# VectorE's reciprocal for the memory rows' softmax factors, and row work moved behind them, in a segment-recurrent attention kernel

## The chip, the cores and the metric

One NeuronCore of a Trainium2 chip runs the whole program. The metric is the time of one execution in microseconds of the device. The kernel before takes 1620.86 us, the median of three executions (1619.89, 1620.86 and 1621.39 us).

## The reference

Four residual steps run over x of 2048 rows by 512 columns: attention with a carried memory (A), a spatially gated MLP (B), A again, B again. The change touches A alone. Cut to what matters:

```python
for s in range(n_seg):                       # 64 segments of 32 rows
    h = concatenate([mem, xs])               # 8 memory rows ahead of the 32 token rows
    q, k, v = h @ Wq, h @ Wk, h @ Wv         # 32 heads of 128 columns
    p = softmax(where(mask, q @ k.T * scale, -1e9))
    o = (p @ v) @ Wo                         # over all heads
    mem = o[:8]                              # the next segment's memory
    outs.append(o[8:])
```

A segment can't begin before the eight memory rows of the segment ahead of it have gone through the softmax, through p @ v and through Wo. There are two blocks A, so 128 segments in a row. In the last segment of each block nothing follows on the memory rows; 126 segments have a step for them.

## The kernel before, in words

**Tiling.** `a_block` builds one block A and calls `segment` 64 times. The 32 heads stand as two halves, r = 0 (heads 0 to 15) and r = 1 (heads 16 to 31). In each half, 8 pairs of heads fill 128 partitions, and a score tile has 224 columns. The tiles of a segment that matter here:

- `E[:, r]`: the masked exponentials of half r, written by VectorE in `close(r)` (L980).
- `psO[0]` and `psO[1]`: the products p @ v of the two halves in PSUM, written by TensorE in `pv(r)` (L1020, L1023). The tile of the second half also holds the sums of the exponentials for the memory rows: `sums[0]`, made ahead of `pv(0)` by `sums_ahead` (L1003), lies in columns 384 to 511 of the first bank of `psO[1]`; `sums[1]`, made after `pv(1)` by `sums_memory` (L994), lies in columns 320 to 383 of both banks. `pv(1)` therefore writes over the bank in which `sums[0]` stands.
- `Rm[:, r]`: the softmax factors 1/sum of the memory rows in SBUF, 128 partitions by 128 fp32 elements.
- `psT`: the sums of the token rows, made by `sums_tokens` (L1012). Their factors `Rt` come later, in `token_factors` (L1087, L1090).
- `uT`: the scaled rows as TensorE takes them for Wo, 32 heads wide.

**The step of the change** is `memory_out(r, ps)` at L1035. It takes the sums to their inverses by exp(-ln(sum)): a Ln on ScalarE from PSUM to `Rm` (L1037), then an Exp with scale -1 on `Rm` in place (L1038). VectorE then multiplies the eight memory rows of `psO[r]` by `Rm` into `uT` (L1039).

**Order of the work.** Each engine runs its instructions in the order in which the program text issues them (a manual schedule for TensorE, VectorE and ScalarE; the DMA issues of SyncE and GpSimd follow the text as well). There is no planner; the order is written out by hand in `segment`. Around the change it reads:

1. `exps(1)`, the copy of the second half's values to `VA` on VectorE (L1075), `close(1)`, then `spare0()`, a hook in which VectorE may do row work of the block's other stages.
2. `fill()` (TensorE work of other stages: projections `psb` of the next 128 rows, or rows of `pwB`), `sums_ahead`, `fill()`, `pv(0)`.
3. `memory_out(0, sums[0])`.
4. `spare1(E)`, a second hook with row work.
5. `pv(1)`, `sums_memory(1)`, `sums_tokens`.
6. `memory_out(1, sums[1])`.
7. `run(copies)` (ScalarE's evictions of the fill work), then `wo_pairs` (L808: heads 0 to 17 into `px`, 36 matmuls) and `wo_rest` (L815: heads 18 to 31 into a part of `psO[0]`). Heads 16 and up need `memory_out(1)`.
8. ScalarE's copy `cross` (L1132), `token_factors`, the hook `spare2`, VectorE's `fold` (L906, L909) and `build_hA` (L916, L917), which writes the memory rows of the next segment into `hT`. The next segment's projections `psQ`, `psm`, `psK`, `psV` (all L731) follow.

**What `spare1` holds.** By segment it is nothing, or one or two of: half of a row block's sum (`rows.y_half`, VectorE L240, with a store issued by GpSimd at L242) or half of its statistics (`y_stats`, VectorE L150); in every fourth segment the next row block's normalisation (`rows.apply`, VectorE L207, with a transposing DMA issued by SyncE at L211); in a few segments the release of finished rows (VectorE L1227 with a store by SyncE); near the end of a block also GpSimd's row sums (L230), and a memset (L1232) with a weight load by GpSimd.

Of the kernel before, what the change touches and what calls it, by code (L numbers as in the profile page):

```python
# [9 lines left out]
ACT = mybir.ActivationFunctionType  # L10
# [662 lines left out]
def a_block(tc, c, rows, front, MV_in, RS_in, MV_out, RS_out, ahead, wo, S, first):  # L673
    nc = tc.nc
    NSEG = S // SEG
    NB = S // P
    scale = float(DH) ** -0.5
    maskN, ones, half = c["maskN"], c["ones"], c["half"]

    with ExitStack() as ctx:  # L680
# [86 lines left out]
        def run(todo):  # L767
            while todo:
                todo.pop(0)()
# [101 lines left out]
        def y_stats(tb, k):  # L871

            if k == 0:
                halves[tb] = rows.pool.tile([P, 2, nc.vector.BN_STATS_DIM], F32, name="bnst2")
            _half_stats(nc, halves[tb], rows.y[tb][0], k, MV_out[:, tb, :])
            if k == 2:
                copies.append(lambda: _rstd_act(nc, RS_out[:, tb:tb + 1], MV_out[:, tb, 1:2], c))
# [47 lines left out]
        def segment(s, fill, spare0, spare1, spare2, spare3, tail, loads):  # L925
# [11 lines left out]
            E = segp.tile([P, 2, 2, 224], BF16, name="E", bufs=1)  # L937
# [88 lines left out]
            def oview(r, lo, hi):  # L1026
                return psO[r][:, :, 0:320].rearrange("p g (n q) -> p g n q", q=40)[:, :, :, lo:hi]

            def hview(t, r, lo, hi):
                return t.rearrange("p (r g n) q -> p r g n q", r=2, g=2)[:, r, :, :, lo:hi]  # L1030
# [3 lines left out]

            def memory_out(r, ps):  # L1035
                rm = Rm[:, r]
                nc.scalar.activation(out=rm, in_=ps, func=ACT.Ln)  # L1037
                nc.scalar.activation(out=rm, in_=rm, func=ACT.Exp, scale=-1.0)  # L1038
                nc.vector.tensor_tensor(out=hview(uT_cur[:], r, 24, 32), in0=oview(r, 0, 8), in1=rm.rearrange("p g (n q) -> p g n q", q=8), op=ALU.mult)  # L1039

            def tok_out(r):
# [41 lines left out]
            ends_here = s + 1 == NSEG  # L1083
            Rt = segp.tile([P, 2, 512], F32, name="Rt", tag="Rt", bufs=1)

            def token_factors(rs):
                nc.scalar.activation(out=Rt[:], in_=psT[:], func=ACT.Ln)  # L1087
                for r in rs:
                    rt = Rt[:, :, 256 * r:256 * r + 256]
                    nc.scalar.activation(out=rt, in_=rt, func=ACT.Exp, scale=-1.0)  # L1090

            def between():
                if first and s == 0:
                    fill()
                    run(turns)
# [7 lines left out]
            pv(0)  # L1103
            if not ends_here:
                memory_out(0, sums[0])
            spare1(E)
            between()
            pv(1)
            if not ends_here:
# [2 lines left out]
            if ends_here:  # L1112
                spare2()
                token_factors((1, 0))
            else:
                memory_out(1, sums[1])
            run(copies)
            px = accB.tile([P, 512], F32, name="px")
            pw = psO[0][:, 0, 384:512]
# [62 lines left out]
        def y_load(y, o):  # L1182
            rows.y_load(y, first, nc.gpsimd, rows.pool.tile([P, DM], F32, name="y_x")[:], o)()
# [8 lines left out]
        for s in range(NSEG):  # L1192
# [19 lines left out]
            def spare1(E):  # L1212
                for y, added in ys:
                    if added:
                        y_stats(y, 1)
                    elif tb < NB - 1:
                        if j4 < 3:
                            rows.y_half(y, first, 1, nc.gpsimd)
                    else:
                        nc.gpsimd.tensor_copy(seen[:], E[:, 1, 0, 0:1])  # L1220
                        rows.y_add(y, first, nc.gpsimd, nc.gpsimd)
                if s == NSEG - 1:
                    y_load(NB - 5, rows.pool.tile([P, DM], F32, name="y_o")[:])
                    rows.y_add(NB - 5, first, nc.gpsimd, nc.gpsimd)
                if stores and not ys:
                    last = yB[max(yB)][:, 0:1]
                    nc.vector.tensor_copy(last, last)  # L1227
                    run(stores)
                if j4 == 3 and tb + 2 < NB:
                    rows.apply(tb + 2, MV_in, RS_in, first=first)  # L1230
                if s == NSEG - 2:
                    nc.vector.memset(front.w_in_sb[:, 2, FH - 1:FH + 1], 0.0)  # L1232
                    front.load_w(2)

            def spare2():
                if first and s == 8:
                    c["cast_bsp"] = c["load_bsp"]()
                if first and s == 12:
                    c["cast_bsp"]()
                for y, added in ys:  # L1240
                    if not added and tb < NB - 1 and j4 == 3:
                        rows.y_half(y, first, 1, nc.gpsimd)
                if (first or tb + 2 >= LATE_STATS) and j4 in (1, 2) and tb + 2 < NB:
                    x_stats(tb + 2, j4 - 1)
# [26 lines left out]
            def loads():  # L1271
                if due and s < NSEG - 1 and (not ys or tb == NB - 1):
# [7 lines left out]
                    else:  # L1280
                        y_load(y, wo.VX[0][:].rearrange("p j r e -> p (j r e)").bitcast(F32))

            segment(s, lambda n=1: [next(more, None) for _ in range(n)], spare0, spare1, spare2, spare3, tail, loads)
        assert due == [NB - 5] and ys == [[NB - 6, True]]
        for k in range(3):
# [58 lines left out]
```

## Time and profile before

| | |
|---|---|
| median of three executions | 1620.86 us (1619.89 to 1621.39) |
| the profiled execution's own time | 1620.98 us |
| its span in the profile | 1619.3 us, 94188 instructions |
| granted TensorE clock | 0.997 |
| TensorE matmul (PE) busy | 1572.9 us, 97% of the span |
| VectorE (DVE) busy | 1215.1 us, 75% |
| ScalarE (ACT) busy | 1064.7 us, 66% |
| GpSimd (POOL) busy | 286.4 us, 18% |

The span begins with the first instruction that the profile holds and ends with the last; the execution's own time is 1.7 us longer. A row of the timeline gives the start and the length in us, then the engine, the line of the kernel, the operation, the tile that it writes and, behind the arrow, what it reads, with their shapes (partitions by elements) and the number of instructions merged into the row. A bracket at the end gives the idle time of the engine ahead of it and who ended it. In a view of groups, the columns behind the count are the busy time of all together in us, the mean of one in ns, and the idle time ahead of them. A view of waits gives who waited for whom: us in total, times, longest. PE is matmuls, PEld the weight loads that run beside them. The ends of matmuls are modelled, so rows of PE overlap a little, and a start is surer than an end.

### The profile page before, as it was taken

Reading aid. Unit: us, or ns where it says so; the run is one execution under the profiler, and the core shown is the slowest. Engines: PE = TensorE matmul, PEld = TensorE weight load, DVE = VectorE, ACT = ScalarE, POOL = GpSimd, SP = SyncE. Lnnn points to the kernel's source line nnn. Section 1 sums busy time; section 2 is a strip of 40 time slices with the busy share of each in tenths; the row PEclk is TensorE's granted clock in tenths of the full one; section 3 lists DMA queues with packets and bytes.
Section 4 is the critical chain, followed back from the end, with each engine's and each line's share of the span. In section 5 each row is a group of like instructions: output and inputs, shape, how many; then the busy total and the mean of one; then the engine's idle time right before and its main releaser. Section 6 shows DMA issues by size and latency. Waiting matters only on the chain.

```text
span 1619.3 us, 94188 instructions
## 1 busy us (share of the span) xinstructions
PE 1572.9 (97%) x42526; PEld 1000.3 (62%) x42526; DVE 1215.1 (75%) x3181; ACT 1064.7 (66%) x2277; POOL 286.4 (18%) x604
## 2 busy tenths in 40 slices
PE   5899999999999999999999999999999999999999
PEld 2566666666666666666656666666666666665565
DVE  4787777878888887884467777777888788877722
ACT  3677777777777777661047777777777777776400
POOL 5111111112211221320011111111121112214000
PEclk8999999999999999999999999999999999999999
DMA  9222122223322343297952221222333233526698
GB/s 370 68 44 45 45 43 44 44 43 81 85 47 44 86 92 72 88 189 151 212 168 50 49 47 47 47 47 47 73 90 72 48 73 92 88 62 174 141 190 170
DMA packets 261851, 148.44 MB, mean 92 GB/s; under 512 B 196425, under 2 KB 238001, under 8 KB 261449
## 3 DMA queue, kind: packets, MB, share of 16 engines
q1 hardware_dynamic: 248184, 98.59, 28.9%
q0 software_dynamic: 12976, 42.77, 8.7%
q8 instruction: 333, 5.46, 1.5%
q10 hardware_dynamic: 288, 1.05, 0.2%
q14 instruction: 70, 0.57, 0.1%
HBM read 59.42 MB, written 36.93 MB: 60 GB/s over the span
## 4 chain that ended last, share of the span: by engine, by line
PE 90%; DMA 4%; DVE 3%; ACT 1%; issue 1%; POOL 0%; SPq 0%; DVEq 0%
PE psQ L731 13%; PE psK L731 13%; PE psb L731 9%; PE pg L398 9%; PE px L808 9%; PE psm L731 7%; PE psV L731 6%; PE psO L815 6%; PE pz L298 3%; PE psO L1020 3%; PE pwB L827 3%; PE py L441 3%; PE psT L1012 2%; PE psS L968 2%; PE psO L1003 1%; PE psO L1023 1%
## 5 line engine op out<-in xcount | busy, mean ns | idle before, releaser
L731 PEld LDWEIGHTS <-hT 128*32 128x32 bf16 x14172 | 372.6, 96 | 284.6 <-DVE hT L917 65.5
L945 DVE STREAM_TRANSPOSE QQ<-rows 128x512 bf16<-128x512 bf16 x256 | 179.7, 702 | 19.5 <-ACT rows L942 11.9
L945 DVE STREAM_TRANSPOSE KA<-rows 128x512 bf16<-128x512 bf16 x256 | 176.4, 689 | 13.1 <-ACT rows L942 12.4
L398 PE MATMUL pg<-z,wspT 128*128 128x344 bf16 x1024 | 154.3, 309 | 0.0
L942 ACT CAST rows<-psQ 128x512 bf16<-128x512 f32 x256 | 142.2, 584 | 17.8 <-PE psQ L731 16.8
L1042 DVE TENSOR_TENSOR uT<-psO,Rt 128x384 bf16<-128x384 f32 x256 | 141.5, 553 | 13.6 <-ACT Rt L1090 5.9
L1090 ACT ACTIVATE Rt<-Rt 128x512 f32<-128x512 f32 x256 | 147.2, 622 | 4.1
L977 ACT ACTIVATE S<-psS 128x224 bf16<-128x224 f32 x256 | 91.4, 357 | 84.6 <-PE psS L972 84.6
L731 PE MATMUL psQ<-Wq_sb,hT 128*32 128x512 bf16 x2048 | 135.4, 381 | 9.0 <-ACT Rt L1087 6.3
L1039 DVE TENSOR_TENSOR uT<-psO,Rm 128x128 bf16<-128x128 f32 x252 | 73.4, 291 | 93.3 <-ACT Rm L1038 50.4
L808 PEld LDWEIGHTS <-uT 128*32 128x32 bf16 x4608 | 111.6, 96 | 47.2 <-DVE uT L1039 33.7
L808 PE MATMUL px<-Wo,uT 128*32 128x256 bf16 x3840 | 134.5, 274 | 2.1 <-DVE uT L1039 1.9
L731 PE MATMUL psV<-Wv_sb,hT 128*32 128x256 bf16 (+1 forms) x2420 | 134.3, 346 | 1.5 <-issue 1.5
L731 PE MATMUL psQ<-Wk_sb,hT 128*32 128x512 bf16 x2048 | 134.9, 381 | 0.0
L1087 ACT ACTIVATE Rt<-psT 128x1024 f32<-128x1024 f32 x128 | 131.0, 1024 | 5.5 <-PE psT L1012 2.5
L731 PE MATMUL psK<-Wk_sb,hT 128*32 128x512 bf16 (+1 forms) x2832 | 134.6, 320 | 0.0
L731 PE MATMUL psK<-Wv_sb,hT 128*32 128x512 bf16 (+1 forms) x2776 | 134.5, 323 | 0.0
L731 PE MATMUL psm<-Wq_sb,hT 128*32 128x512 bf16 x2048 | 134.1, 379 | 0.0
L398 PEld LDWEIGHTS <-wspT 128*128 128x128 bf16 x1024 | 100.1, 98 | 53.2
L815 PE MATMUL psO<-Wo_high,uT 128*32 128x128 bf16 x7168 | 123.7, 219 | 2.5 <-DMA Wo_high<-in_A_Wo_dram 2.5
L900 POOL COPY KX<-old 128x128 bf16<-128x128 bf16 x128 | 68.2, 549 | 320.8 <-PE psS L972 247.0
L900 POOL COPY KX<-front 128x128 bf16<-128x128 bf16 x126 | 64.5, 540 | 310.8 <-PE psS L972 247.3
(203 smaller groups left out, 2911.1 us busy)
## 6 DMA issues: line engine op xcount, KB each, us to landing
o_d<-o_sb SPq DMA_DIRECT2D x126, 64.0 KB
vb_d<-front SPq DMA_DIRECT2D x29, 256.0 KB
VX<-vb_d SPq DMA_DIRECT2D x116, 64.0 KB
ln_x<-xd SPq DMA_DIRECT2D x26, 256.0 KB
y_o<-o_d POOLq DMA_DIRECT2D x22, 256.0 KB, 3.9
xd<-y_o POOLq DMA_DIRECT2D x22, 256.0 KB, 2.7
Wk_sb<-in_A_Wk_dram POOLq DMA_DIRECT2D x8, 512.0 KB, 10.0
Wv_sb<-in_A_Wv_dram POOLq DMA_DIRECT2D x8, 512.0 KB, 11.3
```

What stands on the lines that cost most here:

```text
L398: nc.tensor.matmul(pg[t][:, k, 0:344], lhsT=wsp[t][:, st, :], rhs=z(st, 344 * k, 344 * k + 344), start=(st == 0), stop=(st == NT - 1))
L731: mms.append(nc.tensor.matmul(ps[32 * cg:32 * cg + 32, n * k:n * k + n], lhsT=lhs(kt, cg), rhs=r[:, m * k:m * k + m], start=(kt == 0), sto ...
L808: nc.tensor.matmul(px[at:at + 32, 0:256], lhsT=lhs[:, h, :], rhs=wo_rhs(h, slice(k + 2, None, -2) if h % 2 else slice(k, None, 2)), start= ...
L815: nc.tensor.matmul(pw[32 * cg:32 * cg + 32, :], lhsT=lhs[:, h, :], rhs=wo_rhs(h, cg), start=False, stop=(h == H - 1), tile_position=(0, 32 ...
L900: eng.tensor_copy(KX[:, :, r].rearrange("p g (k i) -> p i g k", i=4), bs["KTB"][:, r].rearrange("p (i g) k -> p i g k", i=4)[:, :, :, 8 * ...
L942: return r, mms, nc.scalar.copy(r[:], ps)
L945: nc.vector.transpose(out=QQ[:, j % 2, :, 0:32] if j < 2 else KA[:, j % 2], in_=r[:])
L977: return nc.scalar.activation(out=S[:, r], in_=psS[:, r, 0:224], func=ACT.Exp, scale=scale)
L1039: nc.vector.tensor_tensor(out=hview(uT_cur[:], r, 24, 32), in0=oview(r, 0, 8), in1=rm.rearrange("p g (n q) -> p g n q", q=8), op=ALU.mult)
L1042: nc.vector.tensor_tensor(out=hview(uT_nxt[:], r, 0, 24), in0=oview(r, 8, 32), in1=rview(r, 0, 24), op=ALU.mult)
L1087: nc.scalar.activation(out=Rt[:], in_=psT[:], func=ACT.Ln)
L1090: nc.scalar.activation(out=rt, in_=rt, func=ACT.Exp, scale=-1.0)
```

## The change

`memory_out` takes the inverse of the sums in one VectorE instruction that reads PSUM and writes `Rm`; the two ScalarE instructions go. And in all segments but the last of a block, `spare1(E)` is issued after `memory_out(1, ...)` and no longer between `memory_out(0, ...)` and `pv(1)`.

```diff
             def memory_out(r, ps):
                 rm = Rm[:, r]
-                nc.scalar.activation(out=rm, in_=ps, func=ACT.Ln)
-                nc.scalar.activation(out=rm, in_=rm, func=ACT.Exp, scale=-1.0)
+                nc.vector.reciprocal(out=rm, in_=ps)
                 nc.vector.tensor_tensor(out=hview(uT_cur[:], r, 24, 32), in0=oview(r, 0, 8), in1=rm.rearrange("p g (n q) -> p g n q", q=8), op=ALU.mult)
...
             pv(0)
             if not ends_here:
                 memory_out(0, sums[0])
-            spare1(E)
+            if ends_here:
+                spare1(E)
             between()
             pv(1)
...
                 token_factors((1, 0))
             else:
                 memory_out(1, sums[1])
+                spare1(E)
             run(copies)
```

## The prediction

> **What bounds the kernel now.** The page's totals and its chain of the work that ended last come first:
>
> ```profile
> PE 1572.9 (97%) x42526; PEld 1000.3 (62%) x42526; DVE 1215.1 (75%) x3181; ACT 1064.7 (66%) x2277; POOL 286.4 (18%) x604
> ...
> PE 90%; DMA 4%; DVE 3%; ACT 1%; issue 1%; POOL 0%; SPq 0%; DVEq 0%
> ```
>
> TensorE sets the end: 90% of the chain is its own work, ScalarE has 1% of it. What the change takes off ScalarE is thus worth nothing unless TensorE waits for it, and every delay of a TensorE instruction in a segment is paid in full, since the next segment needs this one's memory rows. The timelines of TensorE, ScalarE and VectorE in one segment, without row work around the factors, show who waits:
>
> ```profile
> 620.88 0.82 PE L731 MATMUL psb<-Wq_sb,hB 128*32 128x512 bf16 x12
> 621.63 0.32 PE L1020 MATMUL psO<-E,VA 64*128 64x80 bf16 x8
> 621.78 0.22 PE L1023 MATMUL psO<-E,VX 64*128 64x128 bf16 x2
> 621.84 0.31 PE L1020 MATMUL psO<-E,VA 64*128 64x80 bf16 x8
> 621.98 0.22 PE L1023 MATMUL psO<-E,VX 64*128 64x128 bf16 x2
> 622.04 0.22 PE L994 MATMUL psO<-E,ones 64*128 64x64 bf16 x4
> 622.10 0.44 PE L1012 MATMUL psT<-E,ones 64*128 64x512 bf16 x4
> 622.47 1.05 PE L808 MATMUL px<-Wo,uT 128*32 128x256 bf16 x30
> 623.25 0.39 PE L808 MATMUL px<-Wo_high,uT 128*32 128x256 bf16 x6
> 623.46 0.73 PE L815 MATMUL psO<-Wo_high,uT 128*32 128x128 bf16 x40
> ```
> ```profile
> 621.12 0.28 ACT L1037 ACTIVATE Rm<-psO 128x128 f32<-128x128 f32 x1
> 621.43 0.31 ACT L1038 ACTIVATE Rm<-Rm 128x128 f32<-128x128 f32 x1
> 622.30 0.28 ACT L1037 ACTIVATE Rm<-psO 128x128 f32<-128x128 f32 x1 [0.57 <-PE psO L994]
> 622.61 0.31 ACT L1038 ACTIVATE Rm<-Rm 128x128 f32<-128x128 f32 x1
> 622.83 0.57 ACT L793 CAST rowsB<-psb 128x512 bf16<-128x512 f32 x1
> 623.68 0.26 ACT L1132 COPY cross<-px 64x128 f32<-64x128 f32 x1 [0.28 <-PE px L808]
> ```
> ```profile
> 621.25 0.38 DVE L980 TENSOR_TENSOR E<-S,maskN 128x448 bf16<-128x448 bf16 x1
> 622.12 0.29 DVE L1039 TENSOR_TENSOR uT<-psO,Rm 128x128 bf16<-128x128 f32 x1 [0.48 <-PE psO L1023]
> 622.96 0.29 DVE L1039 TENSOR_TENSOR uT<-psO,Rm 128x128 bf16<-128x128 f32 x1 [0.55 <-ACT Rm L1038]
> 623.68 0.28 DVE L906 COPY cross<-px 64x128 f32<-64x128 f32 x1 [0.44 <-PE px L808]
> ```
>
> Three things are to be read from it. First, ScalarE has finished reading the first sums at 621.40, so `pv(1)` (621.84), which writes over their bank, doesn't wait: its 0.21 us behind `pv(0)` (621.63) are `pv(0)`'s own. Second, from `pv(1)` to `px` (622.47) TensorE takes 0.63 us; the first product, done at 622.41, is just in time (some 0.05 us from VectorE's end to TensorE's start). Third, `px`'s 36 matmuls take 0.99 us (622.47 to 623.46), so head 16, behind 32 of them, is wanted at 622.47 + 32/36 x 0.99 = 623.35; the second product is done at 623.25, with the 0.05 us to TensorE some 0.05 us early. The ScalarE pair lies beside TensorE's work, with little to spare and nothing lost.
>
> **The change part by part.** *Removed:* the pair on ScalarE, in 126 segments twice: 252 x (0.28 + 0.31) = 149 us. Nobody gains it as such: ScalarE's next piece on the path, `cross`, waited for `px` (the 0.28 us in its bracket), not for the pair.
>
> *Added:* a reciprocal of the same 128 x 128 elements from PSUM on VectorE, 252 times. No row shows one. Bounds:
>
> ```profile
> L1042 DVE TENSOR_TENSOR uT<-psO,Rt 128x384 bf16<-128x384 f32 x256 | 141.5, 553 | 13.6 <-ACT Rt L1090 5.9
> ...
> L1039 DVE TENSOR_TENSOR uT<-psO,Rm 128x128 bf16<-128x128 f32 x252 | 73.4, 291 | 93.3 <-ACT Rm L1038 50.4 <-PE psO L1023 39.2
> ...
> L135 DVE TENSOR_TENSOR nq<-nq,nt 128x6 f32<-128x6 f32 x12 | 2.0, 166 | 0.4
> ```
>
> One pass over 128 elements costs (553 - 291)/(384 - 128) x 128 = 131 ns on 160 ns that don't grow (166 ns for six elements agree). The lower end is one pass, 0.29 us. The nearest row in kind is VectorE's only inverse in this kernel, the inverse root at L127 to L137 (L135 is one of its rows): a start value, two preparing instructions and three rounds of three, twelve passes, 160 + 12 x 131 = 1.73 us if the element went through them in one instruction: the upper end. A plain inverse needs the start value and, per round, two passes: 1 + 3 x 2 = 7 passes, **1.08 us**, which I take: between ends so far apart it is the nearest row's recipe, less what 1/x has no use for. With two rounds it is 5 passes, 0.82 us; with three passes a round, 10, 1.47 us. These bound my forecast; one and twelve are rivals.
>
> [...]
>
> *Where it lies, first half.* Call its length R. VectorE is in `close(1)` from 621.25 to 621.63 and can start its next instruction about 0.08 us before that ends, at 621.55 (the row further down shows just that offset). The reciprocal ends at 621.55 + R, and now `pv(1)` waits for it, as it read the bank: 621.60 + R in place of 621.84, so TensorE loses R - 0.24 = 0.84 us. Behind `pv(1)` wait `sums_memory`, `sums_tokens` and `px`, so all of it is lost. `px` comes at 622.47 + 0.84 = 623.31; the first product (0.03 us behind the reciprocal, as L1038 stands behind L1037; 0.29 us long) is done at 622.95 and isn't late.
>
> *Second half.* ScalarE began L1037 0.46 us behind `pv(1)`. The reciprocal likewise: 622.68 + 0.46 = 623.14, ends 624.22; the product (0.03 + 0.29 us) follows to 624.54, TensorE sees it at 624.59. Head 16 is wanted at 623.35 + 0.84 = 624.19. Loss: 0.40 us, written with R: R - 0.68, from R = 0.68 on. Both halves: 2R - 0.92, 1.24 us at R = 1.08.
>
> *Row work ahead of the first reciprocal.* `spare0` stands on VectorE between `close(1)` and it:
>
> ```profile
> 611.25 0.38 DVE L980 TENSOR_TENSOR E<-S,maskN 128x448 bf16<-128x448 bf16 x1
> 611.55 0.42 DVE L150 BATCH_NORM_STATS2 bnst<-y_o 128x6 f32<-128x256 f32 x1
> ```
>
> It starts 0.30 us after `close(1)` and holds the reciprocal 0.42 - 0.08 = 0.34 us longer. Before, this fell into the idle time ahead of the product.
>
> ```profile
> L150 DVE BATCH_NORM_STATS2 bnst<-y_o 128x6 f32<-128x256 f32 x40 | 16.5, 418 | 0.0
> L240 DVE TENSOR_TENSOR y_o<-y_o,y_x 128x256 f32<-128x256 f32 x32 | 14.5, 452 | 3.7 <-DMA y_o<-o_d 3.4
> ...
> L207 DVE TENSOR_SCALAR ln_xn<-ln_x,MV,RS 128x512 bf16<-128x512 f32 x14 | 8.1, 579 | 0.0
> ```
>
> Half of the 40 and of the 32 stand in `spare0`: 36 segments, 36 x 0.34 = 12 us.
>
> *Moved:* `spare1`. It no longer stands ahead of the second reciprocal but between the second product and L906. `px` can end only 0.05 us and four matmuls after that product, and L906 follows: 0.05 + (623.68 - 623.35) = 0.38 us. With 0.08 us of overlap one piece of 0.42 us just fits; L207's 0.58 us (14 places), or a second piece behind it (the 16 second halves of L240), is up to 0.2 us late: 30 x 0.2 = 6 us. Its DMAs pass no other issue: between the old place and the new one only TensorE's work stands in 125 of 126 segments, so SP's and POOL's order stays. The transposing DMA behind L207 comes some 2 us later, of which 1.24 us is the segment's own delay. It feeds `hB`:
>
> ```profile
> 605.72 0.29 POOL L640 COPY hB<-hT 128x128 bf16<-128x128 bf16 x1 [0.76 <-DMA hT<-ln_xn]
> ...
> 610.52 0.10 PEld L731 LDWEIGHTS <-hB 128*32 128x32 bf16 x4
> ```
>
> It has 4.5 us before TensorE reads it, so I price this at nothing; without that cover it would be the other 0.8 us at each L207.
>
> *Sum:* 126 x 1.24 = 156 us, 12 us and 6 us: 174 us. The profiled execution took 1620.98 us (0.12 us above the median), so **1795 us**. VectorE is not the bound by its total: 1215.1 + 252 x 1.08 = 1487 us of it.
>
> **The rivals.**
>
> *A. One pass.* The reciprocal runs like any other instruction, 0.29 us. Then `pv(1)` is 0.05 us late, the second product is early, and what is left is 126 x 0.05 = 6 us and the 12 us of `spare0`: 1639 us. For it: every elementwise row here fits one pass. Against it: no row here shows a division, and an inverse of full precision took this kernel many steps.
>
> [...]
>
> *B. Faster: ScalarE was the bound.* Two rows of the waits bear on it and on C:
>
> ```profile
> PEld L1020 <- ACT Rm L1037: 48.8, 115, 0.4
> ...
> PE psQ L731 <- ACT Rt L1087: 6.3, 10, 0.6
> ```
>
> The second is a wait of the next segment's first matmuls for ScalarE. If the pair's removal let L1087 start earlier at those ten places, and the reciprocal were short, the time would be 1620.98 - 6.3 = 1615 us. It decides from R below 0.24 us, where `pv(1)` no longer waits, and only with `spare0`'s 12 us hidden as well; a single pass is already 0.29 us, and ScalarE stands idle ahead of `cross` as it is.
>
> *C. `pv(0)` waits too.* If the first of those rows (weight loads of `pv`) is a true wait of `pv(0)` for the reading of the sums, all 0.21 us of `pv(0)` come behind the reciprocal as well: 126 x 0.21 = 26 us more, 1821 us. Against it: `pv(0)` writes the other tile, and the matmuls ahead of it (620.88 + 0.82) run right up to it.
>
> *D. Twelve passes,* R = 1.73 us: 126 x 2.54 + 18 = 338 us, 1959 us.
>
> That the change doesn't do what it says could be seen only in the order of row work; were `spare1` still ahead of the second reciprocal, it would cost some 0.1 us at 60 places, 6 us.
>
> **How the numbers follow.** Forecast 0.76 and C 0.08, A 0.10, B 0.02, D or longer 0.04. The forecast's own bounds are 5 passes, 126 x 0.72 + 18 = 109 us, and 10 passes, 126 x 2.02 + 18 = 273 us: 1730 to 1894 us. C lies within. That is 0.84 of the chance, so A, B and D, the far ends of the unknown price, stay outside the range, with 0.16. Less than 0.2%, 3.2 us, can't be told from no change; only B is faster by more: faster 0.02, within 0.01, slower 0.97.
>
> **What would show it.** The reciprocal's row: 252 instructions, near 1.08 us each (0.29: A). `pv(1)` begins 0.05 us behind the first reciprocal's end and about 1.05 us behind `pv(0)`; if `pv(0)` itself has moved against L731, C. A gap inside `px` ahead of head 16, 0.4 us, ended by L1039. Segments with row work in `spare0` longer by 0.34 us more. ScalarE 149 us less busy and its idle time longer. The prediction is wrong if R lies outside 0.82 to 1.47 us, or if TensorE's two waits don't add up.

## The result and the profile after

The changed kernel takes 1766.43 us (median of four, 1764.64 to 1767.59), the kernel before 1620.53 us (four, 1619.89 to 1621.39): a ratio of 1.0895, with a 95% interval of 1.0873 to 1.0917. It is slower by 146 us where the prediction had 174 us more: inside its range (1730 to 1894 us) and 29 us below its forecast of 1795 us. The profiled execution took 1764.64 us, 143.66 us more than that of before.

The page of the changed kernel, in the lines that answer to those of before (busy time by engine; the chain of the work that ended last):

```profile
PE 1618.0 (92%) x42526; PEld 988.1 (56%) x42526; DVE 1443.3 (82%) x3433; ACT 936.4 (53%) x1773; POOL 285.9 (16%) x604
...
PE 63%; DVE 28%; ACT 4%; issue 2%; DMA 2%; POOL 0%; SPq 0%; DVEq 0%; ACTq 0%; POOLq 0%
DVE Rm L1037 13%; PE psQ L731 12%; PE psK L731 12%; PE pg L398 8%; PE psm L731 6%; DVE VA L1074 5%; PE psO L815 4%; DVE E L980 4%; PE psb L731 4%; PE pz L298 4%; PE psO L1020 2%; PE py L441 2%; DVE uT L1038 2%; PE px L808 2%; ACT S L977 2%
```

VectorE's share of the chain has gone from 3% to 28%, and the reciprocal (L1037) is its largest single line. ScalarE is 128 us less busy, and that bought nothing. The chain changes owner although VectorE is still only 82% busy: the new work isn't much of the total, but it stands at a place where TensorE waits. The groups of the changed kernel (busy us, mean ns, idle time ahead) give the price that no row of before had:

```profile
L1037 DVE RECIPROCAL Rm<-psO 128x128 f32<-128x128 f32 x252 | 240.0, 952 | 16.3
```

0.952 us for 128 elements a partition: more than three times the 0.291 us of one pass, less than the 1.08 us of the forecast. Where it is paid, the waits tell (us in total, times, longest):

```profile
ACT cross L1133 <- PE px L808: 357.0, 125, 4.8
...
PE psO L1020 <- DVE Rm L1037: 94.5, 126, 2.1
...
PEld L808 <- DVE uT L1038: 81.4, 245, 0.4
...
PEld L1020 <- ACT S L977: 49.7, 117, 0.4
```

The second line is new: once in each of the 126 segments TensorE's matmuls of `pv` wait for the reciprocal. The first shows that ScalarE only waits longer: its wait for `px` was 56.9 us before and is 357.0 us. The timeline of one segment of the same kind as the prediction's, first TensorE, then VectorE:

```profile
551.32 0.32 PE L1020 MATMUL psO<-E,VA 64*128 64x80 bf16 x8
551.48 0.22 PE L1023 MATMUL psO<-E,VX 64*128 64x128 bf16 x2
552.24 0.32 PE L1020 MATMUL psO<-E,VA 64*128 64x80 bf16 x8 [0.55 <-DVE Rm L1037]
552.38 0.24 PE L1023 MATMUL psO<-E,VX 64*128 64x128 bf16 x2
552.44 0.24 PE L994 MATMUL psO<-E,ones 64*128 64x64 bf16 x4
552.50 0.45 PE L1012 MATMUL psT<-E,ones 64*128 64x512 bf16 x4
552.88 1.05 PE L808 MATMUL px<-Wo,uT 128*32 128x256 bf16 x30
553.66 0.69 PE L808 MATMUL px<-Wo_high,uT 128*32 128x256 bf16 x6
554.17 0.73 PE L815 MATMUL psO<-Wo_high,uT 128*32 128x128 bf16 x40
```
```profile
550.94 0.38 DVE L980 TENSOR_TENSOR E<-S,maskN 128x448 bf16<-128x448 bf16 x1
551.24 0.95 DVE L1037 RECIPROCAL Rm<-psO 128x128 f32<-128x128 f32 x1
552.29 0.29 DVE L1038 TENSOR_TENSOR uT<-psO,Rm 128x128 bf16<-128x128 f32 x1
552.72 0.96 DVE L1037 RECIPROCAL Rm<-psO 128x128 f32<-128x128 f32 x1
553.71 0.29 DVE L1038 TENSOR_TENSOR uT<-psO,Rm 128x128 bf16<-128x128 f32 x1
```

`pv(0)` begins at 551.32, the reciprocal ends at 552.19, `pv(1)` begins at 552.24: 0.92 us behind `pv(0)` in place of 0.21, a loss of 0.71 us. From `px` to L815 it is 1.29 us (552.88 to 554.17) in place of 0.99: the second product ends at 554.00, and the four matmuls of heads 16 and 17 follow it. Together that is 1.01 us. With row work ahead of the first reciprocal, VectorE's timeline of another segment reads:

```profile
677.02 0.38 DVE L980 TENSOR_TENSOR E<-S,maskN 128x448 bf16<-128x448 bf16 x1
677.32 0.42 DVE L150 BATCH_NORM_STATS2 bnst<-y_o 128x6 f32<-128x256 f32 x1
677.66 0.94 DVE L1037 RECIPROCAL Rm<-psO 128x128 f32<-128x128 f32 x1
```

The reciprocal begins 0.64 us behind the start of `close(1)` in place of 0.30 us: the 0.34 us are just what the row work occupies. Summed over the starts of 126 segments in both traces, `pv(1)` is 106 us later against `pv(0)`, `px` takes 38 us longer up to head 16, and `fold` begins 6 us later against the end of `px`; 5 us come back between `fold` and the next segment's `pv(0)`.

### The profile page after: what moved, and what is told of

It reads as the page before. It is cut to its first block, busy times and chain, and to the rows that moved or that the text cites. A ratio compares the mean times of both kernels' runs of the same rounds, so it can differ in the third digit from the quotient of the medians.

```text
span 1762.9 us, 93885 instructions
## 1 busy us (share of the span) xinstructions
PE 1618.0 (92%) x42526; PEld 988.1 (56%) x42526; DVE 1443.3 (82%) x3433; ACT 936.4 (53%) x1773; POOL 285.9 (16%) x604
## 4 chain that ended last, share of the span: by engine, by line
PE 63%; DVE 28%; ACT 4%; issue 2%; DMA 2%; POOL 0%; SPq 0%; DVEq 0%; ACTq 0%; POOLq 0%
DVE Rm L1037 13%; PE psQ L731 12%; PE psK L731 12%; PE pg L398 8%; PE psm L731 6%; DVE VA L1074 5%; PE psO L815 4%; DVE E L980 4%; PE psb L731 4%; PE pz L298 4%; PE psO L1020 2%; PE py L441 2%; DVE uT L1038 2%; PE px L808 2%; ACT S L977 2%
## 5 line engine op out<-in xcount | busy, mean ns | idle before, releaser
L731 PEld LDWEIGHTS <-hT 128*32 128x32 bf16 x14172 | 359.8, 97 | 303.4 <-DVE hT L917 78.0
L1037 DVE RECIPROCAL Rm<-psO 128x128 f32<-128x128 f32 x252 | 240.0, 952 | 16.3
L1133 ACT COPY cross<-px 64x128 f32<-64x128 f32 x126 | 33.1, 263 | 357.1 <-PE px L808 357.0
L1020 PE MATMUL psO<-E,VA 64*128 64x80 bf16 x2048 | 81.2, 200 | 94.5 <-DVE Rm L1037 94.5
L1020 PEld LDWEIGHTS <-VA 64*128 64x128 bf16 x2048 | 56.1, 96 | 160.1 <-issue 105.8
```

Of the source, the lines that this page charges most:

```text
L731: mms.append(nc.tensor.matmul(ps[32 * cg:32 * cg + 32, n * k:n * k + n], lhsT=lhs(kt, cg), rhs=r[:, m * k:m * k + m], start=(kt == 0), sto ...
L1020: nc.tensor.matmul(o, lhsT=VA[64 * g:64 * g + 64, r, i, :], rhs=E[64 * g:64 * g + 64, r, :, 40 * i:40 * i + 40], start=(i == 0), stop=True ...
L1037: nc.vector.reciprocal(out=rm, in_=ps)
```

## The experiments

On the chips of the experiments the kernel before took 1615.5 to 1616.1 us, so ratios to it are compared across chips, not bare times.

**The two parts of the change, one at a time.** First the reciprocal with `spare1` left at its old place:

```diff
             def memory_out(r, ps):
                 rm = Rm[:, r]
-                nc.scalar.activation(out=rm, in_=ps, func=ACT.Ln)
-                nc.scalar.activation(out=rm, in_=rm, func=ACT.Exp, scale=-1.0)
+                nc.vector.reciprocal(out=rm, in_=ps)
```

> The reciprocal alone, spare1 left where it was, between the first product and pv(1). Theory of the two waits: the first wait stays as in the changed kernel; the second reciprocal now stands behind spare1's row work, which has only about 0.2 us of room (first product ended to second reciprocal begun), so some 60 segments lose another 0.2 to 0.3 us at head 16, 15 us, and the 6 us of row work late for the fold come back: 1766 + 9 = 1775 us, 1770 to 1782. Rival, the moved row work is part of what costs: clearly below 1766, 1755 or less.

Measured: 1765.54 us, ratio 1.0930 (1.0914 to 1.0946). The time lies below the expected range, but its base was the first chip's 1620.5 us: by the ratio it is 6 us above the changed kernel's 1.0895, inside the range, with intervals that overlap. So the move of the row work is no part of the cost; whether it saves the 9 us, this run alone can't tell.

The changed kernel and this one were then run together on one chip.

> The changed kernel once more, so that the three other runs have it on their own chip: 1.0895 times the kernel before, 1.087 to 1.092.

> The reciprocal alone, spare1 left where it was, once more, now beside the changed kernel on one chip. In the first run's profile the row work costs 7 us more at head 16 than in the changed kernel and 7 us less at the fold. Theory of the two waits, the move is a wash: within 4 us of the changed kernel. Rival, the move is what it claims to be, a help to the second product: 7 us or more above the changed kernel.

Measured: 1765.67 us, ratio 1.0921 (1.0891 to 1.0951), and 1765.06 us, ratio 1.0921 (1.0898 to 1.0944). The changed kernel's ratio is a shade above the 1.092 expected and 0.0026 above that of its first chip, within the intervals: a comparison by ratios across chips is good to some 4 us, not better. On one chip the move is a wash beside the reciprocal. By the starts in the two traces, with the row work at its old place `px` takes 7 us longer up to head 16 (0.1 us at some 60 places, where I had 0.2 to 0.3), and `fold` begins 7 us earlier. The move by itself:

```diff
             if not ends_here:
                 memory_out(0, sums[0])
-            spare1(E)
+            if ends_here:
+                spare1(E)
...
                 memory_out(1, sums[1])
+                spare1(E)
```

> spare1 moved, Ln and Exp kept on ScalarE. Theory of the two waits: the second product is still done at the same time, row work of 0.42 us behind it just fits ahead of the fold, two pieces or the longer normalisation are 0.1 us late at some 30 places: 1620 to 1626 us. Rival, the moved row work is part of what costs: 1630 us or more. Rival, the new place is better as such (the second product no longer waits behind row work): below 1617 us.

Measured: 1619.08 us, ratio 1.0022 (1.0013 to 1.0032): 3.6 us slower. With ScalarE's pair kept, head 16 comes no sooner (0.2 us over all segments by the starts in the traces), so there was nothing to win, and the row work behind the second product holds up the fold by 5 us in the trace.

**The two halves, one at a time,** row work at the new place in both:

```diff
-                nc.vector.reciprocal(out=rm, in_=ps)
+                if r == 0:                                  # the other kernel: r == 1
+                    nc.vector.reciprocal(out=rm, in_=ps)
+                else:
+                    nc.scalar.activation(out=rm, in_=ps, func=ACT.Ln)
+                    nc.scalar.activation(out=rm, in_=rm, func=ACT.Exp, scale=-1.0)
```

> Reciprocal for the first half's sums alone, Ln and Exp for the second's, row work at the new place. Theory of the two waits: pv(1) waits 0.71 us (0.952 - 0.24) in 126 segments, 90 us, and 12 us with row work ahead of it; head 16 waits for nothing: 1620.5 + 102 = 1723 us, 1715 to 1731. Rival, VectorE's added 240 us count by their amount wherever they stand: half of the 146 us, 1693 us.

> Reciprocal for the second half's sums alone, Ln and Exp for the first's, row work at the new place. Theory of the two waits: pv(1) waits for nothing, head 16 waits 0.29 us in 126 segments, 37 us, and some 6 us of late row work: 1620.5 + 43 = 1664 us, 1655 to 1670. This and the first half alone together make up the 146 us of the whole change. Rival, VectorE's added 240 us count by their amount: half of the 146 us, 1693 us.

Measured: the first half alone 1726.43 us, ratio 1.0684 (1.0668 to 1.0700), 111 us more than before, just past the 94.5 to 110.5 us that its range allowed (it had no term for the moved row work); the second half alone 1657.41 us, ratio 1.0263 (1.0247 to 1.0278), 42 us more. Each has 126 reciprocals of 0.95 us, and one costs more than twice what the other does: VectorE's time doesn't count by its amount. 111 + 42 - 3.6 (the move, which both have) is 149 us, and the whole change cost 1765.67 - 1616.09 = 150 us on its second chip, 146 us on its first. With the first half alone the waits of TensorE are these:

```profile
PE psO L1020 <- DVE Rm L1038: 92.5, 126, 2.1
...
PEld L808 <- DVE uT L1042: 33.4, 126, 0.4
```

The wait of `pv(1)` is there in full (94.5 us in the changed kernel), that of `px` is back at its value of before (33.7 us). With the second half alone, TensorE in one segment:

```profile
502.84 0.32 PE L1020 MATMUL psO<-E,VA 64*128 64x80 bf16 x8
502.99 0.22 PE L1023 MATMUL psO<-E,VX 64*128 64x128 bf16 x2
503.05 0.31 PE L1020 MATMUL psO<-E,VA 64*128 64x80 bf16 x8
503.19 0.22 PE L1023 MATMUL psO<-E,VX 64*128 64x128 bf16 x2
503.25 0.22 PE L994 MATMUL psO<-E,ones 64*128 64x64 bf16 x4
503.31 0.44 PE L1012 MATMUL psT<-E,ones 64*128 64x512 bf16 x4
503.67 1.05 PE L808 MATMUL px<-Wo,uT 128*32 128x256 bf16 x30
504.45 0.70 PE L808 MATMUL px<-Wo_high,uT 128*32 128x256 bf16 x6
504.98 0.73 PE L815 MATMUL psO<-Wo_high,uT 128*32 128x128 bf16 x40
```

`pv(1)` comes 0.21 us behind `pv(0)`, as before; `px` takes 1.31 us to L815. The two waits are separate, and add.

**Is it the bank?** `pv(1)` should wait because the reciprocal still reads the bank that it writes over. Two kernels put the first sums into free columns of the score tile `psS`, whose place in PSUM `psT` takes next:

```diff
-            psT = att.tile([P, 2, 512], F32, name="psT")
-            sums = (psO[1][:, 0, 384:512].rearrange("p (g n) -> p g n", g=2), psO[1][:, :, 320:384])
+            sums = (psS[:, 0, 256:384].rearrange("p (g n) -> p g n", g=2), psO[1][:, :, 320:384])
...
+            psT = att.tile([P, 2, 512], F32, name="psT")
             sums_tokens(psT)
```

> The first half's sums in free columns of the score tile's first bank, no longer in the bank that pv(1) writes; all else as in the changed kernel. Theory, pv(1) waits because the reciprocal still reads its bank: pv(1) no longer waits, and the wait passes on to sums_tokens, whose tile takes the score tile's place in PSUM, 0.26 us later in TensorE's order. There 0.46 us are left, head 16 waits 0.29 us as before, since the second reciprocal now stands behind the first product: 0.75 us a segment in place of 1.02, 34 us below the changed kernel (25 to 40). Rival, pv(1) waits for VectorE for another reason (its values, the second half's mask product, or a count of VectorE's work): no change, within 5 us.

Measured: 1739.67 us, ratio 1.0759 (1.0735 to 1.0783), 26 us below the changed kernel on that chip. `pv(1)` no longer waits, so the place of the first sums, in the tile that it writes, was the cause. The bank by itself isn't shown: the program may order `pv(1)` behind any reader of the tile, and no run declares the part of `pv(1)` that writes the other bank free of the reciprocal. And the edit had a wait of its own, as TensorE's timeline of one segment and the list of waits show:

```profile
686.32 0.39 PE L731 MATMUL psb<-Wq_sb,hB 128*32 128x512 bf16 x4
687.01 0.30 PE L1003 MATMUL psS<-E,half 128*32 128x64 bf16 x16 [0.31 <-ACT S L977]
```
```profile
PE psS L1003 <- ACT S L977: 41.0, 126, 0.5
```

`sums_ahead` now waited for the exponential of the second half, which reads the other bank of the same tile: here the program did order by the tile and not by the bank. The next kernel declares that the two don't depend on each other, as the kernel does elsewhere for banks of one tile (`sums_ahead` returns its matmuls for this):

```diff
-            exps(1)
+            expd1 = exps(1)
...
-                sums_ahead(sums[0])
+                other_bank(sums_ahead(sums[0]), expd1)
```

> The first half's sums in the score tile's first bank once more, and sums_ahead declared free of exps(1), which reads that tile's other bank. In the run before it, sums_ahead waited 0.33 us a segment for that exponential (41 us in all), ahead of pv(0); that wait was of my edit's making. Theory of the two waits, as before: sums_tokens waits 0.46 us for the first reciprocal, head 16 0.29 us for the second, 0.75 us a segment in place of 1.02: 34 us below the changed kernel (25 to 40), ratio to the kernel before near 1.071. Rival, moving the sums only shifts one wait about (VectorE's chain of the two reciprocals and products sets head 16 whatever TensorE does ahead of it): no better than the run before, 1.076.

Measured: 1736.87 us, ratio 1.0744 (1.0722 to 1.0766), which is 29 us below the changed kernel by the ratios (1.0921 - 1.0744, times 1616.09). TensorE in one segment:

```profile
685.70 0.32 PE L1022 MATMUL psO<-E,VA 64*128 64x80 bf16 x8
685.86 0.22 PE L1025 MATMUL psO<-E,VX 64*128 64x128 bf16 x2
685.91 0.31 PE L1022 MATMUL psO<-E,VA 64*128 64x80 bf16 x8
686.05 0.22 PE L1025 MATMUL psO<-E,VX 64*128 64x128 bf16 x2
686.11 0.22 PE L994 MATMUL psO<-E,ones 64*128 64x64 bf16 x4
686.63 0.45 PE L1014 MATMUL psT<-E,ones 64*128 64x512 bf16 x4 [0.29 <-DVE Rm L1039]
687.02 1.05 PE L808 MATMUL px<-Wo,uT 128*32 128x256 bf16 x30
687.80 0.70 PE L808 MATMUL px<-Wo_high,uT 128*32 128x256 bf16 x6
688.33 0.28 PE L815 MATMUL psO<-Wo_high,uT 128*32 128x128 bf16 x8
```

The wait has moved from `pv(1)` to `sums_tokens` (L1014), which begins 0.93 us behind `pv(0)` in place of 0.47, as expected, and `px` takes 1.31 us: 0.80 us in this segment where 0.75 was expected. The gain over the kernel just above is 3 us by the medians, on another chip and with overlapping intervals, and 1.0744 lies nearer to the rival's 1.076 than to the 1.071 expected. From one `pv(0)` to the next, the 81 segments without row work take 0.80 us more than before, where the kernel just above took 0.86; the 34 with row work in `spare0` take 1.10 us more, where it took 1.08. So the rival is right: once `pv(1)` is free, VectorE's own row of reciprocal, product, reciprocal, product sets head 16, and most of the 0.33 us that `sums_ahead` had waited cost nothing. The 0.06 us are what the first reciprocal had begun late for it. VectorE in the two segments, the kernel just above (reciprocal 0.36 us behind the start of `close(1)`), then this one (0.30 us, and from there no gap longer than 0.10 us):

```profile
687.02 0.38 DVE L980 TENSOR_TENSOR E<-S,maskN 128x448 bf16<-128x448 bf16 x1
687.38 0.96 DVE L1037 RECIPROCAL Rm<-psS 128x128 f32<-128x128 f32 x1
```
```profile
685.32 0.38 DVE L980 TENSOR_TENSOR E<-S,maskN 128x448 bf16<-128x448 bf16 x1
685.62 0.95 DVE L1039 RECIPROCAL Rm<-psS 128x128 f32<-128x128 f32 x1
686.67 0.29 DVE L1040 TENSOR_TENSOR uT<-psO,Rm 128x128 bf16<-128x128 f32 x1
686.88 0.95 DVE L1039 RECIPROCAL Rm<-psO 128x128 f32<-128x128 f32 x1
687.87 0.29 DVE L1040 TENSOR_TENSOR uT<-psO,Rm 128x128 bf16<-128x128 f32 x1
```

**What makes the price.** Each reciprocal as two of 64 columns:

```diff
-                nc.vector.reciprocal(out=rm, in_=ps)
+                for g in range(2):
+                    nc.vector.reciprocal(out=rm[:, g], in_=ps[:, g])
```

> Each reciprocal as two instructions of 64 columns. Theory, the price is per element on a fixed part of 0.16 us, (952 - 160)/128 = 6.2 ns an element: 0.56 us a piece, 0.08 us overlapped, 1.03 us for two, so 0.08 us more at each of the two waits: 126 x 2 x 0.08 = 20 us above the changed kernel (14 to 26). Rival, the price is mostly fixed (a start of the divide): near 0.9 us a piece, over 150 us above the changed kernel.

Measured: 1767.66 us, ratio 1.0936 (1.0911 to 1.0962), 2 us above the changed kernel, which the intervals don't separate from nothing. Group and timeline of VectorE:

```profile
L1038 DVE RECIPROCAL Rm<-psO 128x64 f32<-128x64 f32 x504 | 242.9, 523 | 16.3
```
```profile
689.45 0.96 DVE L1038 RECIPROCAL Rm<-psO 128x64 f32<-128x64 f32 x2
690.51 0.29 DVE L1039 TENSOR_TENSOR uT<-psO,Rm 128x128 bf16<-128x128 f32 x1
```

Most of the price goes by elements, so the rival of a large fixed part falls; but the 20 us that I had put on the cut fall too: two pieces together last 0.96 us, about as long as the one.

## Why the prediction was right, step by step

- **The bound.** Right: nothing came of 128 us less of ScalarE (the 149 us of its rows overlapped others in part: in the prediction's segment L793 begins 0.09 us before L1038 ends), and its wait for `px` took them up.
- **The price of the reciprocal.** This term was mis-sized: 1.08 us from the recipe of the inverse root, 0.952 us measured. The difference of 0.128 us counts twice in 126 segments, 32 us, and that is what the forecast of 1795 us had too much; at the measured price its own sum gives 126 x (2 x 0.952 - 0.92) = 124 us, with 12 and 6 us for the row work 1763 us, where the profiled execution took 1764.64 us. The recipe was a way to a number between ends far apart; nothing shows that VectorE works by it, and that it came within 0.13 us is luck as much as method.
- **First wait, R - 0.24.** Right: 0.71 us by the formula, 0.71 us in the segment shown, 111 us for the first half alone (with the move, 3.6 us by itself) where 102 were expected, and gone when the sums lay in another tile.
- **Second wait, R - 0.68.** Right: 0.27 us by the formula, 0.30 us in the segment shown, 42 us for the second half alone with its late row work, where 43 were expected.
- **Row work ahead of the first reciprocal.** Right, 0.34 us in the segment shown. In the trace 34 segments have it where 36 were counted, and in them `pv(1)` is 1.12 us later than before, against 0.72 us in the 81 without: 34 x 0.40 = 13 us where 12 were priced. (In the other 11, `close(1)` itself comes late.) No experiment took it away by itself.
- **The moved row work.** Priced at 6 us, 6 us at the fold in the trace; alone 3.6 us. The prediction put the same 6 us on the old place (0.1 us at 60 places), though only as a sign of a change that doesn't do what it says; the trace has 7 us there. So beside the reciprocal the move is worth nothing.
- **The cover of the moved DMA.** Held: no wait of TensorE for `hB`'s DMA appears, while GpSimd waits for it 164.2 us in place of 106.6.
- **Rivals.** A (one pass, 1639 us) and D (twelve, 1959 us) fall with the row of 952 ns, B with the 1.0895. C (`pv(0)` waits too) falls with the timelines: `pv(0)` begins 0.92 us ahead of `pv(1)`, not with it, and the 48.8 us of weight loads that the list of before put to L1037 stand in that of the changed kernel with 49.7 us, put to another ScalarE instruction: they were no wait for the sums.

No experiment points to a version that beats the kernel before. Every one with a reciprocal is slower, and the cheapest of them (second half alone) by 2.6%.

## What to carry to other kernels

Time taken off an engine is worth what the bounding engine waited for it (here 128 us less of ScalarE bought nothing): look at who released the wait before two instructions are traded for one on another engine. And ask when the reader of a PSUM tile is done with it. In the segments shown, ScalarE read the sums at once and VectorE only after its mask product, 0.43 us later against `pv(0)`; its reading also lasts 0.95 us in place of 0.28. So the tile came free 1.10 us later. TensorE had 0.39 us to spare, and `pv(1)`, with other data in that tile, paid the other 0.71 us. By these numbers the earlier start alone could have saved at most 0.43 us of it. An operation that the trace has never shown should be bounded from both sides and measured by itself first; here its price, counted twice in each of 126 segments, was the whole spread of the forecast.

## What the runs showed of the hardware

VectorE's reciprocal of fp32 takes 952 ns for 128 elements a partition (changed kernel) and 523 ns for 64 (each cut in two): as an estimate from these two, 6.7 ns an element ((952 - 523)/64) and 94 ns besides. The 523 ns are a mean over 504 pieces of 485 to 559 ns. Their 252 pairs keep VectorE busy for 242.9 us, 0.964 us a pair, so a second piece begins some 0.08 us before the first has ended (2 x 0.523 - 0.964). A product of two tensors takes 1.02 ns an element in the kernel before ((553 - 291)/256). The price of the reciprocal is the same within 6 ns from another PSUM tile (953 ns from `psS`, 947 ns from `psO`, with the first sums in the score tile). Two in a row of 64 elements each last 0.96 us together, about as long as the 0.952 us of one of 128, so the cut itself costs almost nothing.
